# Narrower sums over the sequence in a fused attention and mixer kernel: 33 columns a head instead of 66, with a new hand-written order

## The chip, the core and the metric

The kernel runs on one core of one Trainium2 chip. The metric is the device time of one execution in microseconds (us); the kernel before has a median of 216.34 us over three runs (215.99 to 217.02). All arithmetic that matters here is in fp32 or in the faster fp32r form, and each engine (TensorE = PE, VectorE = DVE, ScalarE = ACT, GpSimd = POOL, SyncE = SP for the transfers) works through its own queue in order.

## What is computed

Linear attention with a second-order feature map over 4 batches of 4 heads, 1088 positions and 32 values a head, followed by a token mixer and a channel mixer:

```python
def phi(x):
    a = np.einsum('rd,bhsd->bhsr', S1, x)
    b = np.einsum('rd,bhsd->bhsr', S2, x)
    return np.einsum('bhsi,bhsj->bhsij', a, b).reshape(*x.shape[:-1], r * r)
q_p, k_p = (phi(q), phi(k))
kv = np.einsum('bhsf,bhsd->bhfd', k_p, v)
z = np.sum(k_p, axis=2)
num = np.einsum('bhsf,bhfd->bhsd', q_p, kv)
den = np.einsum('bhsf,bhf->bhs', q_p, z)[..., None] + 1e-06
x = num / den                       # then laid out as (batch, position, 128)
h = np.maximum(xt @ w_tok1, 0.0) @ w_tok2
u = x + h.transpose(0, 2, 1)
out = u + np.maximum(u @ w_ch1, 0.0) @ w_ch2
```

The change concerns `kv` and `z`: the sums over the sequence of 64 features times 32 values and a one.

## The kernel before

Every batch b goes through the same steps, and their names appear in the table ORDER, which is the program: `Plan.run` (L177) walks through it word by word and emits each step, so the order of words sets the order in every engine's queue. A word such as `~7` calls `fill` (L261), which puts that many matmuls of a zero tile into the PE queue where the order expects PE to wait.

- `K0` to `K3`, function `keys` (L425): projections of the keys (`.p`, L436, 64 columns moved), copies (`.c`, ACT), products on the DVE (`.v`, L466, in pieces of 4, 4 and 1 tiles of 128 positions), the sums (`.s`, L483), and the copy into `kvz` (`.kvz`, ACT L493). Batch 0 has the sums in six pieces, `K0.s00` to `K0.s18`; the others have one step.
- In the sums, each head h = 2p + j has nine matmuls, one for each tile of positions: 64 feature columns of `k_p` are the stationary side, and the result goes to partitions 0 to 63 (j = 0) or 64 to 127 (j = 1). The moving side is `v`, which holds 33 columns a head, 32 values and ones. Before, both heads of a pair move all 66 columns of the pair, so half of each result is never read: `blocks` (L491) copies only the head's own 33.
- `Q0` to `Q3`: query features; batch 0 on PE, ACT, DVE and POOL (L574 to L602), later ones through DRAM.
- `A0` to `A3`: `.x` (L692, attention), `.n`, `.r`, `.d` (division on ACT and DVE), `.t` (L752 or L758), `.relu`, `.hT`, `.w` (L874 or L878), `.u` (L783), and `.uh`, `.ul` (L849, L852), the two halves of u.
- `U0` to `U11`, spans of the channel mixer: `.f` (L928), `.h` (L932), `.l` (L935), `.s` (L941), three matmuls each for `.f` and `.s`.
- `w00` to `w32`: weights arrive as doubles and are rebuilt as fp32 by ACT (`.abs`, `.low`), DVE (`.clamp` L293, `.shift` L297, `.merge` L300) and POOL (`.add` L307, L309), then split in halves (`.hi`, `.lo`).
- LOADS is the order in which SP issues the first 25 transfers: `v0` is the values of batch 0, `03` the fourth piece of `w_tok1`, `15` the last of `w_tok2`.

Of the kernel before, what the change touches and what calls it, by code (L numbers as in the profile page):

```python
# [35 lines left out]
LOADS = "00 q0a 02 k0 q0b 01 v0 04 03 13 10 12 11 20 q1 k1 30 31 v1 21 15 14 32 22".split()  # L36
# [36 lines left out]
d12 K0.s10 K0.s14 K0.s18 w01.add d11 d20 K0.kvz ~2 A0.x0 w03.low q1 A0.n0 w10.abs A0.x1 A0.n1 k1 w04.merge A0.r0
A0.d0 d30 w04.low w04.add A0.r1 d31 w10.clamp@dve A0.d1 A0.x2 A0.t0 A0.n2 A0.t1 A0.r2 w03.add w10.shift A0.d2 Q1.p
w12.abs w11.abs w12.low v1 w20.abs w10.merge w12.clamp@dve w11.clamp@dve d21 d15 w10.low Q1.c0 w10.add Q1.c1 w11.low
w12.shift w13.abs d14 w20.clamp@dve d32 Q1.w0 Q1.w1 Q1.w2 w12.merge A0.t2 A0.relu ~2 A0.hT w12.add w30.abs d22
w11.shift w20.shift A0.hTh w11.merge w11.add w13.clamp@dve w20.merge w13.shift w20.low w20.add K1.p K1.c0
w30.clamp@dve K1.c4 w13.low w13.merge w13.add K1.v0 w30.low w20.hi w20.lo@pool w30.shift w30.merge w30.add A0.u0
A0.w0 A0.uh00 A0.u1 K1.c8 A0.ul00 A0.w1 U0.f w21.abs w31.low K1.v4 K1.v8 w21.clamp@dve U0.f U0.f K1.s w21.low
A0.uh11 A0.ul11 U0.h w30.hi w30.lo@pool U0.h U0.l U0.l w21.shift U0.h w31.abs w31.clamp@dve w15.abs U1.f U1.h A0.u2  # L80
w21.merge U0.l U0.s U1.f w21.add w31.shift w31.merge w31.add U0.s U0.s U1.l w22.low w22.abs U1.h U1.l U1.f U0.f
w21.hi w22.clamp@dve w21.lo@pool U1.h U1.l w31.hi w31.lo@pool U0.h w22.shift U0.l U1.s U1.s U1.s w22.merge w22.add
w32.abs U0.f U0.f U1.f w32.clamp@dve w04.hi U0.h U0.l U0.h U1.h w32.low w14.abs U0.s w15.clamp@pool U0.s U0.l
w32.shift w22.hi U0.s U1.f U1.l w32.merge w32.add U1.f U0.f w22.lo@dve U1.h U1.l U1.h U1.l U1.s w14.low w15.shift
U1.s U0.f U0.h w03.hi U0.h w14.clamp@pool U0.l w15.merge U0.l U1.s w14.shift U0.s w32.hi w32.lo@pool Q1.w3 U0.f U0.f
w14.merge w15.low U0.h U0.s w15.add U0.h U0.l w01.hi U0.l U0.f w00.hi U0.h U0.l w02.hi U0.f U1.f w14.add w00.lo@dve
U0.h w10.hi U0.s A0.w2 U1.h U1.l U0.s K1.kvz A0.uh22 U0.l U1.f w15.hi U0.oh@pool U1.h U0.s Q1.r0None Q1.r00 Q1.r01
# [965 lines left out]
```

## Time and profile before

| | value |
|---|---|
| median of the runs | 216.34 us |
| time of the profiled execution | 216.37 us |
| its span, first to last instruction | 213.9 us |
| instructions | 4865 |
| DMA traffic | 28.35 MB, mean 133 GB/s |

The profile divides the span in 40 slices of 5.3 us and lists groups of instructions by source line, the waits between engines and the chain of work that ended last. An fp32 matmul shows as two records on PE, so the 144 matmuls of the sums are 288 records. The stretch up to about 30 us, in which weights are loaded and rebuilt and the first batch goes through attention, is called the head below. Times inside the execution count from the span's start.

### The profile page before, as it was taken

To read this page: it belongs to the slowest core of one execution; us is meant where nothing else is said; L and a number is where in the kernel's file an instruction comes from. 1 tells how busy PE (TensorE), PEld (TensorE's weight loads), DVE (VectorE), ACT (ScalarE), POOL (GpSimd) and SP (SyncE) were. 2 spreads that over 40 slices of the span, in tenths; PEclk is the share of its full clock that TensorE was granted. 3 is DMA by queue.
4 is the path that set the end of the run, shared out by engine and by line. 5 is a ranking of instruction groups with operands and counts; after the bars stand their busy time and mean duration, and the time that the engine had idled before them with its cause. 6 is when DMAs were issued, how large, how long until landed. Compare 5 with 4: busy or idle time off the path is not lost.

```text
span 213.9 us, 4865 instructions
## 1 busy us (share of the span) xinstructions
PE 209.5 (98%) x1876; PEld 199.1 (93%) x1876; DVE 147.1 (69%) x299; ACT 116.2 (54%) x282; POOL 60.9 (28%) x66
## 2 busy tenths in 40 slices
PE   8999999999999999999999999999999999999993
PEld 7779779999998999999999999999999999999993
DVE  2899999998789765777434666585547656556562
ACT  4788997988456245444344544443336453544541
POOL 3177686989971001301000660010000010000000
PEclk9999999999999999999999999999999999999999
DMA  6999985750778598300697400014400200100000
GB/s 223 402 405 409 399 328 129 138 146 10 241 304 242 148 193 171 135 3 3 203 221 184 123 29 0 3 37 142 120 0 0 78 0 0 37 3 37 0 31 25
DMA packets 11398, 28.35 MB, mean 133 GB/s; under 512 B 1520, under 2 KB 5616, under 8 KB 11376
## 3 DMA queue, kind: packets, MB, share of 16 engines
q1 hardware_dynamic: 11232, 27.79, 41.7%
q8 instruction: 14, 0.23, 0.5%
q10 hardware_dynamic: 144, 0.26, 0.5%
q14 instruction: 8, 0.07, 0.1%
HBM read 23.21 MB, written 4.83 MB: 131 GB/s over the span
## 4 chain that ended last, share of the span: by engine, by line
PE 97%; ACT 1%; DVE 0%; issue 0%
PE ps_o L941 34%; PE ps_h L928 33%; PE ps_a L758 5%; PE ps_a L692 4%; PE ps_a L878 4%; PE ps_o L264 3%; PE ps_a L483 3%; PE ps_a L436 2%; PE ps_a L874 2%; PE ps_a L752 1%; PE ps_a L574 1%; PE ps_o L483 1%; PE ps_a L629 1%; PE ps_h L574 1%; PE ps_a L783 1%; PE ps_a L792 1%
## 5 line engine op out<-in xcount | busy, mean ns | idle before, releaser
L935 DVE SCALAR_TENSOR_TENSOR hl<-ps_h,hh 128x384 fp32r<-128x384 f32 (+2 forms) x144 | 74.5, 531 | 46.0 <-ACT hh L932 45.3
L932 ACT ACTIVATE hh<-ps_h 128x384 fp32r<-128x384 f32 (+2 forms) x144 | 67.4, 474 | 63.1 <-PE ps_h L928 54.0
L928 PE MATMUL ps_h<-uh,halves 128*128 128x384 f32 (+2 forms) x288 | 85.4, 330 | 0.0
L941 PE MATMUL ps_o<-hh,halves 128*128 128x384 f32 (+2 forms) x288 | 71.2, 330 | 0.0
L928 PEld LDWEIGHTS ps_h<-uh,halves 128*128 128x128 f32 x288 | 53.1, 188 | 0.6
L941 PEld LDWEIGHTS ps_o<-hh,halves 128*128 128x128 f32 x288 | 50.2, 188 | 0.8 <-issue 0.4
L928 PE MATMUL ps_h<-ul,halves 128*128 128x384 f32 (+2 forms) x144 | 47.1, 327 | 0.0
L941 PE MATMUL ps_o<-hl,halves 128*128 128x384 f32 (+2 forms) x144 | 47.1, 327 | 0.0
L852 POOL TENSOR_TENSOR ul<-us,uh 128x320 fp32r<-128x320 f32 (+4 forms) x10 | 7.2, 727 | 71.1 <-ACT uh L849 71.1
L928 PEld LDWEIGHTS ps_h<-ul,halves 128*128 128x128 f32 x144 | 27.1, 188 | 0.2 <-DVE ul L852 0.2
L941 PEld LDWEIGHTS ps_o<-hl,halves 128*128 128x128 f32 x144 | 27.1, 188 | 0.0
L307 POOL TENSOR_TENSOR whole<-c,tail 128x512 int32<-128x512 int32 (+3 forms) x11 | 11.7, 1072 | 2.7 <-ACT tail L290 1.3
L286 ACT ACTIVATE c<-doubles 128x512 f32<-128x512 f32 (+3 forms) x17 | 10.5, 625 | 3.1 <-DMA doubles<-wt 2.5
L466 DVE TENSOR_TENSOR k_p<-ps_a,a_sb 128x1024 f32<-128x1024 f32 (+1 forms) x12 | 11.0, 947 | 0.0
L722 POOL TENSOR_TENSOR xl<-x,xh 128x384 fp32r<-128x384 f32 x3 | 3.0, 1014 | 26.0 <-ACT xh L718 26.0
L290 ACT ACTIVATE tail<-doubles 128x512 int32<-128x512 uint32 (+3 forms) x17 | 10.4, 625 | 0.0
L300 DVE SCALAR_TENSOR_TENSOR c<-doubles,ps_h 128x512 int32<-128x512 int32 (+3 forms) x17 | 10.3, 609 | 0.2
L297 DVE TENSOR_SCALAR ps_h<-c 128x512 int32<-128x512 int32 (+3 forms) x17 | 10.2, 613 | 0.1
L758 PE MATMUL ps_a<-halves,xh 128*128 128x256 f32 x54 | 9.8, 283 | 0.0
L692 PEld LDWEIGHTS ps_a<-kvz,qp 128*64 128x64 f32 x288 | 8.7, 138 | 0.9 <-issue 0.7
L692 PE MATMUL ps_a<-kvz,qp 128*64 128x66 f32 x288 | 9.3, 223 | 0.0
L264 PE MATMUL ps_o<-still 128*128 128x128 f32 x38 | 8.0, 364 | 1.1 <-DVE still L242 1.1
(85 smaller groups left out, 238.7 us busy)
## 6 DMA issues: line engine op xcount, KB each, us to landing
qp<-rows SPq DMA_DIRECT2D x6, 544.0 KB, 5.0
br<-rows SPq DMA_DIRECT2D x12, 272.0 KB
doubles<-wc SPq DMA_DIRECT2D x6, 512.0 KB, 5.9
v_sb<-v SPq DMA_DIRECT2D x4, 594.0 KB, 10.6
doubles<-wt SPq DMA_DIRECT2D x4, 512.0 KB, 5.4
k_sb<-kT SPq DMA_DIRECT2D x3, 576.0 KB
xm<-xb SPq DMA_DIRECT2D x3, 576.0 KB
xT<-xm SPq DMA_DIRECT2D x12, 144.0 KB, 3.2
```

What stands on the lines that cost most here:

```text
L264: nc.tensor.matmul(spare_ps[:, :P], lhsT=still, rhs=still, start=True, stop=True)
L286: nc.scalar.activation(f32(t["c"]), f32(high), AF.Abs)
L290: nc.scalar.activation(t["tail"], low.bitcast(U32), AF.Copy, scale=2.0 ** -29)
L300: nc.vector.scalar_tensor_tensor(t["c"], high, -(1 << 30), t["ps"], op0=ALU.bitwise_and, op1=ALU.bitwise_or)
L307: engines[e].tensor_tensor(dst(), t["c"], t["tail"], op=ALU.add)
L466: engines["pool" if on_pool else "dve"].tensor_tensor(t["k_p"][:pn, t0 * H:t1 * H], a.unsqueeze(3).broadcast_to([pn, n, R, R]), t["sb", t0 ...
L692: nc.tensor.matmul(x_ps[c:c + 64, o:o + 2 * (D + 1)], lhsT=qp[:, p, s0 + c:s0 + c + 64], rhs=kvz_all[b % 2][:, p, :2 * (D + 1)], start=Tru ...
L758: nc.tensor.matmul(t["h_ps"][:, :DTOK], lhsT=t[l][:m, i, :], rhs=part(0, piece, r, j * DTOK, DTOK)[:m], start=(i == 0 and k == 0), stop=(i ...
L928: nc.tensor.matmul(h_ps[:, :cn], lhsT=part(2, at[2][e][0], l, at[2][e][1] * P, P), rhs=r[:, :cn], start=(m == 0), stop=(m == 2))
L932: nc.scalar.activation(t["hh"][:, :cn], t["h"][:, :cn], AF.Relu)
L935: nc.vector.scalar_tensor_tensor(t["hl"][:, :cn], t["h"][:, :cn], 0.0, f32(t["hh"][:, :cn]), op0=ALU.max, op1=ALU.subtract)
L941: nc.tensor.matmul(outs[i][:, :cn], lhsT=part(3, at[3][e][0], l, at[3][e][1] * P, P), rhs=r[:, :cn], start=(e == 0 and m == 0), stop=(e == ...
```

## The change

The sums move the head's own 33 columns and write them to the head's own 33 columns of the bank. The copy into `kvz` reads the same places as before. The planner's cost for one tile of a pair of heads is changed with it; these costs have no effect where ORDER is given. The table ORDER and the list LOADS are new from the first line to the last:

```diff
-LOADS = "00 q0a 02 k0 q0b 01 v0 04 03 13 10 12 11 20 q1 k1 30 31 v1 21 15 14 32 22".split()
+LOADS = "00 q0a 02 k0 q0b 01 03 04 v0 10 30 11 12 q1 13 20 k1 31 32 21 22 v1 14 15".split()
...
-v0 ~2 K0.s00 K0.s04 Q0.a10 K0.v8 K0.s08 Q0.m10 w01.shift w01.merge d04 d03 Q0.a11 Q0.b11 Q0.m11 w04.abs
...
+w03.clamp@dve v0 Q0.a21 K0.s00 K0.s04 w04.shift Q0.b21 Q0.m21 d10 Q0.a20 Q0.m20 w04.merge w01.add w03.shift
...
                         nc.tensor.matmul(
-                            t["kv"][j * F:(j + 1) * F, p * 2 * (D + 1):(p + 1) * 2 * (D + 1)],
+                            t["kv"][j * F:(j + 1) * F, h * (D + 1):(h + 1) * (D + 1)],
                             lhsT=t["k_p"][:n, i * H + h].rearrange("p i j -> p (i j)"),
-                            rhs=t["v"][:n, i, 2 * p:2 * p + 2, :].rearrange("p h d -> p (h d)"),
+                            rhs=t["v"][:n, i, h, :],
                             start=(i == 0), stop=(i == NT - 1),
                         )
...
-            last = plan.add(f"{n}.s", {"pe": 2 * NT * 117.0}, all_sums, ...
+            last = plan.add(f"{n}.s", {"pe": 2 * NT * 85.0}, all_sums, ...
...
-                    f"{n}.s{p}{t0}", {"pe": (t1 - t0) * 117.0}, sums(p, t0, t1), ...
+                    f"{n}.s{p}{t0}", {"pe": (t1 - t0) * 85.0}, sums(p, t0, t1), ...
```

What the new order does to the queues is shown at three places. The first is PE between the second query projection and the first attention of batch 0. L574 are the query projections, L264 the fills, L483 the sums of batch 0, L692 the attention. Before:

```order
L264 MATMUL ps_o<-still 128x128 x3
L574 MATMUL ps_a<-q_sb,s_spread 128x384 x2
L574 MATMUL ps_h<-q_sb,s_spread 128x384 x2
L264 MATMUL ps_o<-still 128x128 x2
L483 MATMUL ps_o<-v_sb,k_p 64x66 x18
L574 MATMUL ps_a<-q_sb,s_spread 128x320 x2
L574 MATMUL ps_h<-q_sb,s_spread 128x320 x2
L483 MATMUL ps_o<-v_sb,k_p 64x66 x18
L264 MATMUL ps_o<-still 128x128 x2
L692 MATMUL ps_a<-kvz_84,qp 64x66 x36
```

The same place on PE after the change:

```order
L264 MATMUL ps_o<-still 128x128 x2
L574 MATMUL ps_a<-q_sb,s_spread 128x384 x2
L574 MATMUL ps_h<-q_sb,s_spread 128x384 x2
L264 MATMUL ps_o<-still 128x128 x7
L574 MATMUL ps_a<-q_sb,s_spread 128x320 x2
L574 MATMUL ps_h<-q_sb,s_spread 128x320 x2
L483 MATMUL ps_o<-v_sb,k_p 64x33 x36
L264 MATMUL ps_o<-still 128x128 x2
L692 MATMUL ps_a<-kvz_84,qp 64x66 x36
```

The half of the sums that stood ahead of the third query projection now follows it, and seven fills stand where two fills and that half stood.

The second place is the DVE around the first reciprocal (L704) of batch 0; L293, L297 and L300 are conversions of weights, L712 a division. Before:

```order
L300 SCALAR_TENSOR_TENSOR c<-doubles_94,ps_h 128x512
L300 SCALAR_TENSOR_TENSOR c<-doubles_93,ps_h 128x256
L704 RECIPROCAL rec<-den 128x12
L712 TENSOR_TENSOR x<-ps_a,rec 128x384
L704 RECIPROCAL rec<-den 128x12
```

And after:

```order
L300 SCALAR_TENSOR_TENSOR c<-doubles_93,ps_h 128x512
L293 TENSOR_SCALAR c<-c 128x384
L704 RECIPROCAL rec<-den 128x12
L712 TENSOR_TENSOR x<-ps_a,rec 128x384
L704 RECIPROCAL rec<-den 128x12
```

One clamp of 384 columns has come ahead of the reciprocal; before, it follows it.

The third place is the DVE ahead of the first `ul` (L852), with which the channel mixer can begin; L466 are products of the keys of batch 1. Before:

```order
L300 SCALAR_TENSOR_TENSOR c<-doubles_95,ps_h 128x384
L466 TENSOR_TENSOR k_p<-ps_a,a_sb 128x1024
L297 TENSOR_SCALAR ps_h<-c 128x512
L300 SCALAR_TENSOR_TENSOR c<-doubles_100,ps_h 128x512
L852 TENSOR_TENSOR ul<-ps_a,uh 128x384
```

And after:

```order
L466 TENSOR_TENSOR k_p<-ps_a,a_sb 128x1024
L293 TENSOR_SCALAR c<-c 128x512
L297 TENSOR_SCALAR ps_h<-c 128x512
L466 TENSOR_TENSOR k_p<-ps_a,a_sb 128x256
L300 SCALAR_TENSOR_TENSOR c<-doubles_96,ps_h 128x512
L852 TENSOR_TENSOR ul<-ps_a,uh 128x384
```

The small product of 256 columns now stands ahead of `ul`; before, it follows. The clamp of 512 columns stands ahead of `ul` in both, before the change a few rows earlier. On PE, two fills more stand ahead of the second pair of L874 matmuls (`A0.w1`), and the sums of batch 1 stand right behind the third group of L783 instead of apart from it. After the head PE keeps the same work in another interleaving.

More of the change, by code (lines that the diff above doesn't have):

```diff
@@ L73 @@
[L73 to L87, printed above, removed]
@@ L123 @@
-U10.l U10.f U10.s U10.h U10.l U10.f U10.h U10.l U10.l U10.f U10.s U10.l U11.f U10.s U10.s U10.h U10.l U11.f U10.s
-U11.f U11.h U11.h U11.h U11.l U11.l U10.s U11.s U11.f U11.f U11.s U10.ol U10.out U11.l U11.h U11.h U11.f U11.h U11.s
-U11.l U11.f U11.l U11.f U11.s U11.s U11.l U11.s U11.f U11.h U11.h U11.l U11.f U11.s U11.l U11.f U11.s U11.h U11.h
-U11.l U11.l U11.f U11.s U11.h U11.h U11.s U11.l U11.l U11.s U11.s U11.ol U11.out
+s k0a s.abs s.clamp s.shift s.low s.merge s.add s.rows ~4 K0.p0 d00 w00.abs q0a w00.clamp@dve Q0.s0@pool Q0.s1@pool
@@ new lines @@
+~1 Q0.p0 d02 K0.c0 K0.v0 w00.low w02.abs k0 ~1 K0.p4 w00.shift w02.low Q0.a00 w02.clamp@dve w00.merge w00.add Q0.a01
+Q0.b01 q0b K0.c4 K0.c8 d01 w01.abs w01.low Q0.m00 ~2 Q0.p1 Q0.m01 Q0.a10 w02.shift K0.v4 w02.merge w02.add Q0.a11
+Q0.b11 Q0.m11 w01.clamp@dve K0.v8 d03 d04 w04.abs w03.abs Q0.m10 w03.low w01.shift w01.merge ~7 Q0.p2 w04.clamp@dve
+w03.clamp@dve v0 Q0.a21 K0.s00 K0.s04 w04.shift Q0.b21 Q0.m21 d10 Q0.a20 Q0.m20 w04.merge w01.add w03.shift
+w03.merge d30 d11 w03.add d12 q1 d13 K0.s08 K0.s10 w10.abs w10.clamp@dve K0.s14 K0.s18 K0.kvz ~2 A0.x0 w04.low A0.x1
@@ new lines @@
+w22.hi w22.lo@pool U1.f U1.h U1.h U0.f U0.h w14.clamp@dve U1.l U1.l w15.shift U0.l w15.merge w15.add U1.s U1.s U0.f
+U0.h w14.shift w12.hi U0.l w14.merge w14.add U1.s U0.s U0.f U0.f w32.hi U0.f U0.h w32.lo@dve K1.kvz U0.h w10.hi U0.h
+U0.l U0.s U0.s U0.f U0.h U0.l U1.f U0.l U0.oh@dve A0.w2 Q1.w0 Q1.w1 Q1.w2 Q1.w3 w03.hi Q1.r0None Q1.r00 Q1.r01
+Q1.r1None Q1.m10@pool Q1.r10 Q1.r11 w11.hi U0.l q2 U1.f k2 Q1.m11@pool v2 q3 U0.s U1.f U1.h A0.uh22 U1.h U0.s U0.s
+U1.l A0.ul22 U1.f U1.h w04.hi Q1.m01@dve w01.hi U1.h Q1.m00@pool w02.hi A1.x U1.l U1.f U1.l U1.l w02.lo@pool A1.n1
@@ L522, in all_sums @@
                     sums(p, 0, NT)(_)
-            last = plan.add(f"{n}.s", {"pe": 2 * NT * 117.0}, all_sums, products + [v_loaded[b]], [kv_hold], [kp_hold, v_hold[b]], boost, 1)
+            last = plan.add(f"{n}.s", {"pe": 2 * NT * 85.0}, all_sums, products + [v_loaded[b]], [kv_hold], [kp_hold, v_hold[b]], boost, 1)
         for p in () if b else range(2):
```

89 lines of the change are left out of this document (49 added, 40 removed).

## The prediction

> **What bounds the kernel now.** I read the page first, then the chain of work that ended last, then the timeline of the head. The page's busy shares, and PE and DVE in 40 slices of 5.3 us:
>
> ```profile
> PE 209.5 (98%) x1876; PEld 199.1 (93%) x1876; DVE 147.1 (69%) x299; ACT 116.2 (54%) x282; POOL 60.9 (28%) x66
> PE   8999999999999999999999999999999999999993
> DVE  2899999998789765777434666585547656556562
> GB/s 223 402 405 409 399 328 129 138 146 10 241 304 242 148 193 171 135 3 3 203 221 184 123 29 0 3 37 142 120 0 0 78 0 0 37 3 37 0 31 25
> ```
>
> PE is busy all along, but in the head that share deceives, since fills count as busy there. DVE is at 9 tenths or near it over the first eight slices, and the transfers run at some 400 GB/s until 27 us. So the head is set by several engines together, and the rest by PE alone. Whatever PE saves behind the head is time saved; what it saves inside the head counts only where DVE waits for it.
>
> The chain, in order of time (start, length, line, records), where the sums (L483) and their neighbours stand:
>
> ```profile
> 9.41 0.86 PE ps_o L264 x6
> 10.28 0.84 PE ps_a L574 x4
> 11.12 0.65 PE ps_h L574 x4
> 11.77 0.64 PE ps_o L264 x4
> 12.41 1.20 PE ps_o L483 x36
> 13.61 0.74 PE ps_a L574 x4
> 14.35 0.54 PE ps_h L574 x4
> 14.89 1.20 PE ps_o L483 x36
> 16.09 0.64 PE ps_o L264 x4
> 16.73 2.25 PE ps_a L692 x72
> ...
> 31.12 2.25 PE ps_a L483 x72
> 33.37 0.72 PE ps_h L928 x3
> ...
> 34.94 0.52 PE ps_h L928 x3
> ...
> 55.85 2.25 PE ps_a L692 x72
> ...
> 62.21 1.20 PE ps_a L436 x36
> ...
> 66.86 2.25 PE ps_a L483 x72
> 69.12 1.05 PE ps_a L436 x36
> ...
> 99.43 2.25 PE ps_a L483 x72
> ```
>
> **What a sum costs, and what sets its pace.** 36 records cost 1.20 us and 72 cost 2.25, so 36 more cost 1.05: 29.2 ns a record, or 58.3 for a pair, one record on each half of the partitions, side by side. Four batches take 2.40 + 3 x 2.25 = 9.15 us. Would half the columns be half of that? L436, the projections of the keys, tells:
>
> ```profile
> L436 PE MATMUL ps_a<-s_blocks,k_sb 128*64 128x64 f32 x144 | 5.7, 235 | 0.0
> L483 PE MATMUL ps_a<-v_sb,k_p 128*64 128x66 f32 x216 | 7.0, 223 | 0.0
> ```
>
> The form 128*64 is the weights' rows and columns, 128x64 or 128x66 what is moved. L436 has the same 64 columns of weights and moves 64 columns, not 66. Its 36 records cost 1.20 with the entry, like those of the sums, and 1.05 right behind the sums. If the moved columns set the pace, 36 records would take 1.05 x 64/66 = 1.02, a difference of 0.03 that rows of two decimals would show. It isn't there, so something common to both sets the pace: 64 columns of weights. The sums in the third batch, and L629 ahead of them, give the size of that (min, median, max in ns):
>
> ```profile
> L483 PE MATMUL ps_a<-v_sb,k_p x72: 220/222/273, 66.8 to 68.9; 128*64 128x66 f32 x72
> ...
> L629 PE MATMUL ps_a<-q_sb,s_rows x16: 387/403/418, 66.2 to 66.5; 64*32 64x272 f32 x16
> ```
>
> The record that begins a block waits for its own weights with nothing to cover them: 273 - 222 = 51 ns for 64 columns, and about 418 - 387 = 31 for 32. In the middle of a block one load must end before the next can start, so 51 ns a pair is a floor whatever is moved, and 58.3 is what a pair takes. I bound the new pair from both sides: 58.3 (weights set the pace throughout) and 58.3 x 33/66 = 29.2 (moved columns do after all). Between them stands 51. I take 58.3, because the equality of 64 and 66 columns speaks for it and the floor of 51 lies near it. Each block may end one narrower record earlier, at most 0.03 us.
>
> TensorE: Matmul & The Clock Gate of the Trainium skill, Part 3, on what overlaps, says that a weight load overlaps a matmul in flight only where the two use different groups of rows; all pairs here use all 128 rows. By that rule load and moved columns would add up, and 33 columns fewer would save the full 29.2 ns a pair, the extreme of the first rival below; the trace speaks against it, since a load of 51 plus 66 columns would need over 58.3.
>
> **The head.** First the PE queue, which now has one fill less, the second query projection, seven fills, the third projection, all sums, two fills, attention. The rows that the start of each piece depends on, from the timeline:
>
> ```profile
> 12.78 0.54 DVE L602 TENSOR_TENSOR qp<-xT,ps_h 128x384 f32<-128x384 f32 x1
> 16.14 0.43 ACT L493 COPY kvz<-ps_o 64x66 f32<-64x66 f32 x2 [0.44 <-PE ps_o L483]
> 17.84 0.23 DVE L704 RECIPROCAL rec<-den 128x12 f32<-128x12 f32 x1 [0.39 <-ACT den L700]
> 18.78 0.30 DVE L293 TENSOR_SCALAR c<-c 128x384 f32<-128x384 f32 x1
> 12.45 0.41 DVE L466 TENSOR_TENSOR k_p<-ps_a,a_sb 128x256 f32<-128x256 f32 x1
> 27.67 0.31 PEld L783 LDWEIGHTS ps_a<-ident,x 128*128 128x128 f32 x3 [0.49 <-DVE k_p L466]
> 28.85 0.55 DVE L852 TENSOR_TENSOR ul<-ps_a,uh 128x384 fp32r<-128x384 f32 x1
> ```
>
> And the stretch up to `ul` in the view by windows (busy us and instructions of PE, PEld, DVE, ACT and POOL, then clock, DMA share and GB/s):
>
> ```profile
> 5.80:28.85 23.05, 23.00 (x297) 17.16 (x296) 22.33 (x46) 19.15 (x48) 14.55 (x14) 1.00 1.03 403
> ```
>
> Two records of fill are 0.86 - 0.64 = 0.22. The second projection ends at 11.77 or 0.22 earlier. Fourteen fill records are 0.64 + 5 x 0.22 = 1.74, which ends at 13.29 to 13.51. The third projection needs the bank that L602 frees at 12.78 + 0.54 = 13.32, so the fills cover that wait. It runs 0.74 + 0.54 = 1.28, to about 14.7. All sums in one block are 2.25, to 16.95 (two blocks were 2.40). The two fills that cover the copy into `kvz` are 0.64, as before. Attention starts at about 17.6, where it started at 16.73: **+0.85**. Values `v0` now land behind `03` and `04`, 768 KB at 405 GB/s or 1.9 us later; before, they were there at 12.41 at the latest, so now by 14.3, ahead of 14.7. That hides the later load; if the cover goes, the excess goes on top.
>
> Then DVE. It had waited 0.39 for the first `den`; with attention 0.85 later, the reciprocal comes at 18.7. Behind it stand in order the divisions and all conversions up to `ul`, so they all shift. One clamp of 384 (0.30, or 0.22 net, since neighbours overlap by 0.08) is now done inside that wait, and one product of 256 (0.41, 0.33 net) has come ahead of `ul`. The window up to `ul` has DVE busy for 22.33 of 23.05 us, so there is no slack to absorb it. `ul` starts at 28.85 + 0.85 - 0.22 + 0.33 = 29.8: +0.95. PE gives the same: its wait of 0.49 at L783 goes, as PE arrives later than that product, and two new fills (0.43 to 0.64) stand where it was. I take **+0.95** for the start of the channel mixer; from below 0, if the loads that arrive otherwise let DVE and PE catch up, from above 1.6, by the third rival.
>
> **Behind the head.** The shares of the chain by engine:
>
> ```profile
> PE 97%; ACT 1%; DVE 0%; issue 0%
> ```
>
> So a delay at 30 us is carried to the end.
> - Sums of batches 1 to 3: 3 x 36 pairs x (58.3 - 58.3) = 0, and at the ends 4 x 0.03 = 0.1 saved.
> - The block of batch 1 no longer stands alone among L928. A return to L928 cost 0.72 instead of 0.52, so one return fewer saves 0.2.
> - `v1` is issued behind three more loads of 512 KB (`21`, `32`, `22`), 3.9 us at 405 GB/s. It was issued at 16.13 and took 10.6 to land, 26.7, so it lands at 30.6. Its sums start at 31.12 + 0.95 plus some 0.4 for L783 ahead of them: hidden, by 1.8 us.
>
> ```profile
> 16.13 0.33 SPq L268 DMA_DIRECT2D v_sb<-v  x1
> v_sb<-v SPq DMA_DIRECT2D x4, 594.0 KB, 10.6
> ```
>
> - The rows of queries 1, written by SP, now queue behind all loads, up to 32 us. Attention of batch 1 reads them at 55.85 in the chain; hidden.
> - The end keeps its form, a last `.s`, one addition and one transfer: 0.
>
> **The sum**, against the profiled execution's own 216.37 us (a span of 213.9 and 2.47 around it, and 0.03 from the median): 216.37 + 0.95 - 0.1 - 0.2 = **217.0**, a change of +0.3%. A measurement of this kernel tells about 0.5%, or 1.08 us, from no change, so the edges are 215.3 and 217.4.
>
> **Rivals.**
> 1. *The moved columns count after all.* At 29.2 a pair, 36 pairs save 1.05 us a batch: three batches behind the head 3.15, and batch 0 takes the same off the delay of 0.95: 217.0 - 4.2 = 212.8. The planner's cost fell from 117 to 85 for two pairs; 117 is 2 x 58.3, so 85 may have been seen as well. 42.5 a pair would save 36 x 15.8 ns = 0.57 a batch, four times: 217.0 - 2.3 = 214.7, the price I give this rival. For it: that number, and that PE is never idle behind the head. Against it: L436 at the same pace with 64 columns, and 42.5 is less than the 51 of a lone load. Chance 0.28, of which 0.05 for the extreme.
> 2. *A floor of its own.* With 51 a pair, 7.3 ns x 36 x 4 = 1.05: 216.0. TensorEngine Tiling of the Trainium skill, Instruction Overhead, has a matmul of one column as long as one of 60; by it 33 columns would save what 66 to 60 does, 58.3 x 6/66 = 5.3 ns a pair or 0.8 in four batches, and the time would be 216.2. No run here shows so few columns. Chance 0.12, together with a head that catches up (216.1).
> 3. *Slower: the late sums hold up the head further.* The place is the start of attention. If the fills run at the 0.16 a record of the group of four, fourteen take 2.24, not 1.74, and attention starts at 18.1; the two fills ahead of L874 then add their 0.15 to 0.2 in full. The delay is 1.6 instead of 0.95: 217.7. It decides when attention starts after 18.0. For it: the rate of the group of four; against it: the group of six. Chance 0.15.
>
> **How the numbers follow.** The forecast, 216.5 to 217.5, has 0.45. The range goes from 214.4, which takes in most of the first rival, to 217.9, past the third. It leaves out the extreme of the first, 212.8, and a head that loses over 1.7. Faster by over 0.5%: most of the first rival, 0.23. Slower by over 0.5%: the third rival and the upper edge of the forecast, 0.22. The rest, 0.55, is within 0.5%.
>
> **What would show it.** In the changed profile, the 288 records of L483 should stand 29 ns apart, with blocks of 2.2 to 2.3 us; blocks of 1.6 would mean the first rival, 1.9 the second. Attention of batch 0 should start at 17.4 to 17.8, the first reciprocal wait a microsecond, and `ul` start at 29.6 to 30.0. What would make it wrong: a pair faster than 51 ns, attention that starts by 17.0, or a new wait of PE behind 35 us, which I have at none.

## The result, and the profile after

| | before | after |
|---|---|---|
| median of the runs compared | 216.17 us (4 runs) | 218.63 us (4 runs) |
| time of the profiled execution | 216.37 us | 218.56 us |
| its span | 213.9 us | 216.6 us |

The change makes the kernel slower: the ratio is 1.0112, with a 95% interval of 1.007 to 1.0153. The measured time lies 1.6 us above the forecast of 217.0 and 0.7 above its range.

The page after, busy shares and the two rows in slices, and the shares of its chain by engine:

```profile
PE 210.5 (97%) x1888; PEld 199.7 (92%) x1888; DVE 144.4 (67%) x294; ACT 116.6 (54%) x282; POOL 65.9 (30%) x71
PE   8899999999999999999999999999999999999993
DVE  2898999897787554877533866755736755555563
...
PE 90%; DMA 5%; DVE 2%; ACT 1%; issue 0%; SPq 0%
```

PE looks as busy as before. The chain tells more: DMA and DVE now hold 7% of it, where DVE had 0%. Somewhat under half of that stands in the first 9 us, in the loading and rebuilding of the first weights; the rest comes later. The chain of the kernel after, in order of time (start, length, line, records):

```profile
11.79 1.76 PE ps_o L264 x14
...
14.82 2.22 PE ps_o L483 x72
...
17.69 2.25 PE ps_a L692 x72
...
29.62 1.29 PE ps_a L874 x4
30.92 1.82 PE ps_h L928 x9
33.06 2.22 PE ps_a L483 x72
35.28 0.73 PE ps_o L941 x3
...
64.97 6.17 DMA k_sb<-kT
...
71.27 1.27 PE ps_a L436 x36
...
131.37 1.21 DVE qp L672
```

The sums of a batch take 2.22 us, where they took 2.25: half the moved columns, the same block. Attention starts 0.96 later than before, the channel mixer (L928) 1.41 later (30.92 against 29.51). Its piece in the chain before:

```profile
29.51 1.61 PE ps_h L928 x9
```

Then a load of keys and a product on DVE stand in the chain, far behind the head. The chain counts the whole length of such a piece, the 6.17 of the load for example; how long PE waited for it stands in another view. The view of PE's waits from 35 us to the end (engine, line, what it waited for: us in total, times, longest) lists three, and none of them is in the kernel before:

```profile
PE ps_a L436 <- DMA k_sb<-kT: 0.3, 1, 0.3
PE ps_a L483 <- PE ps_a L629: 0.3, 1, 0.3
PE ps_h L928 <- DVE hl L935: 0.2, 1, 0.2
```

To see where time is lost, PE's own work without the fills was added up record by record, each at the usual pace of its kind, and each kernel's time at the same amount of work was set against that of the kernel before. This loss is a number worked out from the traces, for one profiled execution of each kernel. The table gives it at 40 us and at 210 us of the kernel before; "behind" is what was added between. "Time" is the median of all runs of a kernel, "spans" that of the runs less than 1.5% above its fastest. "Old" and "new" are the orders; the head ends where the first channel mixer step begins.

| kernel | time | spans | attention | `ul` | loss at 40 | at 210 | behind |
|---|---|---|---|---|---|---|---|
| before | 216.05 to 216.81 | 214.0 to 214.2 | 16.66 | 28.85 | 0 | 0 | 0 |
| after | 218.63 | 216.7 | 17.62 | 30.47 | 1.58 | 2.76 | 1.18 |
| e1: old order, 33 columns | 216.32 | 213.9 | 16.89 | 29.12 | 0.66 | 0.68 | 0.02 |
| e2: new order, 66 columns | 218.81 | 216.8 | 17.85 | 30.70 | 1.83 | 2.85 | 1.02 |
| h1: old head, new rest | 219.13 | 217.0 | 16.54 | 28.97 | 0.54 | 2.02 | 1.48 |
| h2: new head, old rest | 217.03 | 215.15 | 17.46 | 30.31 | 1.41 | 1.23 | -0.18 |
| g1: k3 later | 218.62 | 216.7 | 17.72 | 30.56 | 1.67 | 2.75 | 1.08 |
| g2: product later | 218.50 | 216.6 | 17.57 | 30.41 | 1.53 | 2.20 | 0.67 |
| g12: both | 218.83 | 216.6 | 17.87 | 30.73 | 1.82 | 2.48 | 0.66 |
| i1: loads behind the store | 218.19 | 216.25 | 16.91 | 29.75 | 0.87 | 1.94 | 1.07 |
| i2: old head, g1, g2, i1 | 217.39 | 215.25 | 17.71 | 29.94 | 1.53 | 2.01 | 0.48 |
| j1: new head, four undone | 218.15 | 216.2 | 17.52 | 30.36 | 1.47 | 2.28 | 0.81 |
| j2: old head, four undone | 217.16 | 215.0 | 16.35 | 28.59 | 0.15 | 0.81 | 0.66 |
| k1: new head, three undone | 217.30 | 215.3 | 17.55 | 30.40 | 1.51 | 1.54 | 0.03 |
| k2: old head, three undone | 216.96 | 214.8 | 16.44 | 30.87 | 3.12 | 3.04 | -0.08 |
| j3: product behind `ul` | 216.87 | 215.1 | 17.57 | 30.21 | 1.34 | 1.18 | -0.16 |
| f1: two fills | 218.97 | 217.05 | 17.14 | 30.55 | 1.66 | 3.43 | 1.77 |
| f2: values earlier | 220.64 | 218.7 | 17.77 | 31.78 | 3.68 | 5.10 | 1.42 |

### The profile page after: what moved, and what is told of

Its sections match the earlier page's. It is cut to its first block, busy times and chain, and to the rows that moved or that the text cites. A ratio compares the mean times of both kernels' runs of the same rounds, so it can differ in the third digit from the quotient of the medians.

```text
span 216.6 us, 4887 instructions
## 1 busy us (share of the span) xinstructions
PE 210.5 (97%) x1888; PEld 199.7 (92%) x1888; DVE 144.4 (67%) x294; ACT 116.6 (54%) x282; POOL 65.9 (30%) x71
## 4 chain that ended last, share of the span: by engine, by line
PE 90%; DMA 5%; DVE 2%; ACT 1%; issue 0%; SPq 0%
PE ps_o L941 32%; PE ps_h L928 32%; PE ps_a L758 4%; PE ps_a L692 4%; PE ps_a L878 4%; DMA k_sb<-kT 3%; PE ps_a L436 2%; PE ps_a L483 2%; DMA doubles<-wt 2%; PE ps_a L752 2%; PE ps_o L264 2%; PE ps_a L874 2%; PE ps_o L483 1%; PE ps_a L574 1%; PE ps_a L783 1%; PE ps_a L629 1%
## 5 line engine op out<-in xcount | busy, mean ns | idle before, releaser
L935 DVE SCALAR_TENSOR_TENSOR hl<-ps_h,hh 128x384 fp32r<-128x384 f32 (+2 forms) x144 | 74.3, 532 | 46.9 <-ACT hh L932 46.3
L928 PE MATMUL ps_h<-uh,halves 128*128 128x384 f32 (+2 forms) x288 | 86.0, 331 | 0.2 <-DVE hl L935 0.2
L941 PE MATMUL ps_o<-hh,halves 128*128 128x384 f32 (+2 forms) x288 | 71.0, 329 | 0.0
L928 PEld LDWEIGHTS ps_h<-uh,halves 128*128 128x128 f32 x288 | 53.0, 188 | 1.3 <-DVE hl L935 0.7
L941 PEld LDWEIGHTS ps_o<-hh,halves 128*128 128x128 f32 x288 | 50.1, 188 | 0.6 <-issue 0.4
L928 PE MATMUL ps_h<-ul,halves 128*128 128x384 f32 (+2 forms) x144 | 47.1, 327 | 0.0
L941 PE MATMUL ps_o<-hl,halves 128*128 128x384 f32 (+2 forms) x144 | 47.0, 327 | 0.0
L928 PEld LDWEIGHTS ps_h<-ul,halves 128*128 128x128 f32 x144 | 27.1, 188 | 0.5 <-DVE ul L852 0.5
L852 POOL TENSOR_TENSOR ul<-us,uh 128x256 fp32r<-128x256 f32 (+4 forms) x11 | 7.9, 720 | 63.6 <-ACT uh L849 63.3
L941 PEld LDWEIGHTS ps_o<-hl,halves 128*128 128x128 f32 x144 | 27.1, 188 | 0.0
L307 POOL TENSOR_TENSOR whole<-c,tail 128x512 int32<-128x512 int32 (+3 forms) x11 | 12.5, 1141 | 9.6 <-DVE c L300 7.8
L466 DVE TENSOR_TENSOR k_p<-ps_a,a_sb 128x1024 f32<-128x1024 f32 (+1 forms) x12 | 11.2, 951 | 0.7 <-ACT a_sb L446 0.7
L409 POOL TENSOR_TENSOR halves<-whole,halves 128x512 fp32r<-128x512 f32 (+3 forms) x9 | 10.0, 1125 | 5.2 <-ACT halves L406 5.2
L297 DVE TENSOR_SCALAR ps_h<-c 128x512 int32<-128x512 int32 (+3 forms) x17 | 10.4, 616 | 0.1
L300 DVE SCALAR_TENSOR_TENSOR c<-doubles,ps_h 128x512 int32<-128x512 int32 (+3 forms) x17 | 10.3, 611 | 0.1
L264 PE MATMUL ps_o<-still 128*128 128x128 f32 x50 | 9.2, 335 | 1.1 <-DVE still L242 1.1
L264 PEld LDWEIGHTS ps_o<-still 128*128 128x128 f32 x50 | 7.9, 235 | 2.4 <-issue 1.1
L722 POOL TENSOR_TENSOR xl<-x,xh 128x384 fp32r<-128x384 f32 x5 | 5.1, 1016 | 15.1 <-ACT xh L718 15.1
```

Of the source, the lines that this page charges most:

```text
L264: nc.tensor.matmul(spare_ps[:, :P], lhsT=still, rhs=still, start=True, stop=True)
L297: nc.vector.tensor_scalar(t["ps"], t["c"], 3, 0x3FFFFFFF, op0=ALU.logical_shift_left, op1=ALU.bitwise_and)
L300: nc.vector.scalar_tensor_tensor(t["c"], high, -(1 << 30), t["ps"], op0=ALU.bitwise_and, op1=ALU.bitwise_or)
L307: engines[e].tensor_tensor(dst(), t["c"], t["tail"], op=ALU.add)
L466: engines["pool" if on_pool else "dve"].tensor_tensor(t["k_p"][:pn, t0 * H:t1 * H], a.unsqueeze(3).broadcast_to([pn, n, R, R]), t["sb", t0 ...
L928: nc.tensor.matmul(h_ps[:, :cn], lhsT=part(2, at[2][e][0], l, at[2][e][1] * P, P), rhs=r[:, :cn], start=(m == 0), stop=(m == 2))
```

## Experiments: sums or order

The change has two parts that do not need each other. Each alone:

```diff
 e1: ORDER and LOADS of before
-rhs=t["v"][:n, i, 2 * p:2 * p + 2, :].rearrange("p h d -> p (h d)"),
+rhs=t["v"][:n, i, h, :],
 e2: ORDER and LOADS of after
-rhs=t["v"][:n, i, h, :],
+rhs=t["v"][:n, i, 2 * p:2 * p + 2, :].rearrange("p h d -> p (h d)"),
```

> The kernel before with its own order and loads; only the sums move 33 columns instead of 66. Theory (64 columns of weights set the pace, so the narrower side is hidden): pairs of records in L483 stay 58.3 ns apart, the time is that of before within 0.3 us, at most 0.1 us less. Rival (the moved columns count somewhere that the changed profile does not show, such as at the ends of the blocks): 215 us or less with before at 216.2.

> The changed kernel with its new order and loads, but 66 columns moved. Theory: the order alone makes the loss, so the time is that of the changed kernel, 218.6 us, within 0.3 us, and pairs stay at 58.3 ns. Rival (the narrower sums save something and the order loses more than the whole): 219.5 us or more.

e1 measured 216.32 us, ratio 0.9978 (0.9943 to 1.0012); e2 218.81, ratio 1.0088 (1.0055 to 1.012). Narrow sums alone gain nothing that shows, and the new order alone makes the loss. In e1 the 36 records of a half batch and the 72 of a batch stand in the timeline (start, length, then the form) as

```profile
15.07 1.24 PE L483 MATMUL ps_o<-v_sb,k_p 128*64 128x33 f32 x36
31.33 2.29 PE L483 MATMUL ps_a<-v_sb,k_p 128*64 128x33 f32 x72
```

so 18 pairs more take 1.05 us: 58.3 ns a pair, as with 66 columns. In the records themselves 33, 64 (L436) and 66 columns all come to 58.33.

## Experiments: what sets the pace of a pair

Two runs change one size of the pair each, in the order of before. e3 is e1, with its 33 moved columns, and takes 32 of the 64 feature columns as weights, so half of the features are left out of the sums. e4 is the kernel before, with all 64, and moves the columns of all four heads.

```diff
 e3
-lhsT=t["k_p"][:n, i * H + h].rearrange("p i j -> p (i j)"),
+lhsT=t["k_p"][:n, i * H + h, :R // 2].rearrange("p i j -> p (i j)"),
 e4
-rhs=t["v"][:n, i, 2 * p:2 * p + 2, :].rearrange("p h d -> p (h d)"),
+rhs=t["v"][:n, i].rearrange("p h d -> p (h d)"),
```

> Only as a measurement of the pace: the order of before, 33 columns moved, and 32 of the 64 feature columns as weights, so that half of the features are left out of the sums. Theory (the load of the weights' columns sets the pace of a pair): the pair falls from 58.3 ns to 29 to 35, and the 72 records of a batch from 2.2 to about 1.2 us. Rival (a fixed pace of some 58 ns for a pair whatever its sizes): 58.3 as before. Second rival (the rows of the weights or the moved columns set the pace, not the weights' columns): 58.3 too, or anything above 45.

> The other side of the same measurement: the order of before, 64 feature columns as weights, and the 132 columns of all four heads moved, of which three heads' are not read. Theory (the slower of weight load and moved columns sets the pace, and 66 columns lie just under the load): the pair rises to 110 to 117 ns, 132 columns at 58.3/66 = 0.88 ns each or somewhat less, and the time by 36 x 4 pairs x 55 ns = 8 us less what the head hides: 222 to 225. Rival (load and moved columns add up, and the equality of 33, 64 and 66 is a floor): above 125. Second rival (a fixed pace whatever is moved): 58.3 and 216.3.

The timeline of e3, a half batch and a batch:

```profile
14.68 0.76 PE L483 MATMUL ps_o<-v_sb,k_p 128*32 128x33 f32 x36
31.17 1.33 PE L483 MATMUL ps_a<-v_sb,k_p 128*32 128x33 f32 x72
```

and of e4:

```profile
16.10 2.25 PE L483 MATMUL ps_o<-v_sb,k_p 128*64 128x132 f32 x36
70.99 4.27 PE L483 MATMUL ps_a<-v_sb,k_p 128*64 128x132 f32 x72
```

With half the weights 18 pairs take 0.57 us, 31.7 ns a pair; with 132 moved columns 2.02 us, 112.2 (112.5 in the records themselves). One run each: 214.31 us for e3 and 224.35 for e4, 8 us above before as expected. So a pair takes the longer of two things: the load of its weights, 31.7 ns for 32 columns and 58.3 for 64, or its moved columns, 112.5 / 132 = 0.85 ns each. By that 66 columns are 56 ns, just under the 58.3 of their weights, which is why the halving found nothing to save. All rivals with a fixed pace, and the one in which load and columns add up, fall.

The rule that the prediction took from TensorE: Matmul & The Clock Gate of the Trainium skill, Part 3, its list of what overlaps (a load overlaps a matmul in flight only where the groups of rows differ), falls with them for this case: all rows are in use in every pair, and 33 columns or 66 make the same 58.3 ns. The floor of some 60 columns in TensorEngine Tiling of the Trainium skill, Instruction Overhead, does not show here either: 33 columns pass in 31.7 ns once the weights let them.

## Experiments: which part of the order

The order was cut at the first step of the channel mixer, and the head of one joined to the rest of the other.

```diff
 h1
 ORDER up to the first U0.f, LOADS: before
+ORDER from the first U0.f: after
 h2
 ORDER up to the first U0.f, LOADS: after
+ORDER from the first U0.f: before
```

Steps that only the other order has ahead of the cut stand right ahead of it: six in h1, three in h2.

> 33 columns. All steps up to the first step of the channel mixer stand in the order of before, with its loads; what is left follows in the new order. Theory (the loss has two parts, 1.6 us in the head and 1.2 us behind it, at the sums of batch 2, the keys of batch 3 and a wait for hl at 133 us): 217.2 to 217.5 us. Rival (the waits behind the head only follow from a head that ends late): 216.2 us, like before.

> 33 columns. The new order and loads up to the first step of the channel mixer, and what is left in the order of before. Theory (two parts): 1.6 us over before, 217.6 to 217.9 us. Rival (all comes from the head): 218.6 us.

h1: 219.13 us, ratio 1.0099 (1.0061 to 1.0137). h2: 217.03, ratio 1.0012 (0.9983 to 1.004), and no wait of PE behind the head. By the spans the new head alone costs about 1.0 (215.15 against 214.2), and the new rest behind it another 1.55 (216.7 against 215.15). The loss is not all in the head. Nor do the two parts simply add: behind the old head the new rest loses 2.8 (217.0 against 214.2), more than behind the new one, with runs from 215.5 to 218.2.

## Experiments: the places behind the head

Three waits are in the profile after, a fourth in that of h1. Moved one by one:

```diff
 g1
-K3.p A1.l1@pool ... K3.c8 A1.t0
+A1.l1@pool ... A1.t0 K3.p K3.c8
 g2
-U5.l Q3.m10@dve U5.l U5.s U5.f U5.l Q3.m01@pool
+U5.l U5.l U5.s U5.f U5.l Q3.m10@dve Q3.m01@pool
 g12: both
 i1
-U0.l q2 U1.f k2 Q1.m11@pool v2 q3 U0.s ... A1.x ... U0.ol ... U0.out
+U0.l U1.f Q1.m11@pool U0.s ... U0.ol U0.out q2 k2 v2 q3 A1.x
 i2: the old head of h1, with g1, g2 and i1
```

> The changed kernel with the first keys step of batch 3 (its projections and its first copy) moved behind the token mixer's first matmul step of batch 1 (.t0), so that PE has its other work to do while the load of k3 is under way. Theory (the wait for k3 near 71 us is a cost of the new order, and nothing behind it is hidden): the 0.3 of wait that L436 has there goes, and with the return to L928 that it forces the time falls by 0.3 to 0.5 us: 218.1 to 218.3 where the changed kernel has 218.6. Rival (the wait only takes the place of the wait for DVE right ahead of it, sums of batch 2 for K2.v8, so PE waits there all the same): within 0.2 of the changed kernel, with a wait of 0.3 or more on DVE or on ps_a in its place between 68 and 75 us.

> The changed kernel with one query product of batch 3 (Q3.m10 on DVE, 1.21 us) moved behind the next two low halves of the channel mixer's hidden values (L935) that it now stands ahead of. Theory (PE's wait at 133 us for hl is due to that product on the DVE queue): the waits of 0.16 on PE and 0.48 on PEld at 133 us go, and the time falls by 0.3 to 0.5: 218.1 to 218.3. Rival (those hl wait for ACT or for PE's own spans, not for the product): the same wait stands, time within 0.2 of 218.6. A second rival: the product in its new place holds up the two hl behind it, and the wait appears some 1.5 us later at the same size.

> Both moves together. Theory (two separate waits of PE, one behind the other on the path): the gains add up to 0.7 to 1.0 us: 217.6 to 217.9. Rival (PE's lost time is made up later whatever the wait, since some later event has a time of its own): the gain of both together is no more than that of the better one alone.

> The changed kernel with the loads of batch 2 and 3 (q2, k2, v2, q3) moved back behind the store of the first span of the channel mixer (U0.out, with its addition U0.ol), both ahead of the attention of batch 1, which is where the kernel before has them in SP's queue. In the changed kernel these loads are issued from 37.4 to 40.6 us, while the rows of the queries of batch 1 are being read, and in the kernel before from 54.3 on. Theory (the loads share the transfers with those reads, and in part of the executions the reads end too late for the attention of batch 1, as in the profiled run with k3 later, which lost 0.38 there): the reads end by 51 us as before, the waits at 53 to 56 us are gone in every run, the time falls by 0.3 to 0.6 to 218.0 to 218.3, and the runs lie within some 1 us of each other, where those of the new order spread over 1.6 to 2.9. Rival (the reads take their 15 us by themselves, being small pieces): they end at 52 as before the move, and the time stays within 0.2 of 218.6. Slower is possible too, if k2 then lands after 64 us, where its projections start.

> Narrow sums, the old head, and the new order behind the head with all three repairs: loads of batch 2 and 3 behind the first store, k3's projections later, the query product of batch 3 later. The old head with the new rest alone has 219.1. Theory (the three places behind the head, queries of batch 1, k3 and the product at 133 us, are the whole loss of the new order's rest): within 0.5 of the kernel before run beside it, 216.0 to 217.0. Rival (the new rest is tight throughout, and each wait taken away lets another appear): 217.5 to 219.0, with waits of PE of 0.2 or more at places that the changed kernel's profile does not show.

**The product (g2).** The time is 218.50, 0.1 below the kernel after, less than hoped and within what the runs can tell. The profile does show the mechanism. The timeline after, DVE, POOL and PE around 133 us:

```profile
129.32 2.68 POOL L672 TENSOR_TENSOR qp<-qp,br 128x544 f32<-128x544 f32 x2 [0.98 <-DMA br<-rows]
131.37 1.21 DVE L672 TENSOR_TENSOR qp<-qp,br 128x544 f32<-128x544 f32 x1
132.50 1.56 DVE L935 SCALAR_TENSOR_TENSOR hl<-ps_h,hh 128x384 fp32r<-128x384 f32 x3
133.10 0.45 PE L928 MATMUL ps_h<-uh,halves 128*128 128x384 f32 x1 [0.16 <-DVE hl L935]
```

and in g2, where the product has moved behind POOL's:

```profile
129.28 2.69 POOL L672 TENSOR_TENSOR qp<-qp,br 128x544 f32<-128x544 f32 x2 [1.05 <-DMA br<-rows]
...
132.82 0.72 DVE L672 TENSOR_TENSOR qp<-qp,br 128x544 f32<-128x544 f32 x1
```

The same product of 544 columns takes 1.21 us beside POOL's and 0.72 behind it. In the first case it ends at 132.58, 0.58 after POOL's pair ends at 132.00; in i1, where it starts earlier, it takes 1.51 and ends 0.57 after. In g1 it starts only 0.25 before POOL's pair ends, takes 0.83, and ends 0.58 after. So it waits for POOL to finish, whenever it starts, and three low halves (L935) queue behind it in the kernel after. SBUF — State Buffer of the Trainium skill, Who interferes with whom, has a DVE instruction with two inputs in SBUF contend with a GpSimd instruction that reads SBUF, and calls the ports that they share an exclusive lock. The trace agrees: 0.72 alone, 0.83, 1.21 and 1.51 together. In the profiles the loss at this place is 0.44 after and 0 in g2; without the move it is 0.05 in g1 and 0.75 in i1, by how early the product starts.

**k3 (g1).** 218.62, nothing gained. g12: 218.83, nothing gained by both. The k3 wait goes, but j1 and k1 below, which differ in this move alone, show that the move itself costs 0.9 of span (216.2 against 215.3).

**The loads (i1).** 218.19, ratio 1.0092 (1.0055 to 1.0129); the spans fall by 0.45, within what was expected. The queue of SP tells why. Before, q2, k2, v2 and q3 stand behind the store of the first span, which waits for the channel mixer:

```profile
53.93 0.36 SPq L977 DMA_DIRECT2D outT<-o_sb  x1
54.34 0.43 SPq L268 DMA_DIRECT2D q_sb<-qT  x1
```

After, they are issued while the rows of the queries of batch 1 are still being read:

```profile
36.15 1.20 SPq L662 DMA_DIRECT2D br<-rows  x2
37.39 0.44 SPq L268 DMA_DIRECT2D q_sb<-qT  x1
```

The profiled execution after does not lose by it. That of g1, with the same four loads in the same place, does; its timeline has POOL waiting for the reads, and PE's weights for POOL:

```profile
52.99 3.17 POOL L672 TENSOR_TENSOR qp<-qp,br 128x544 f32<-128x544 f32 x2 [1.73 <-DMA br<-rows]
...
56.22 2.18 PEld L692 LDWEIGHTS ps_a<-kvz,qp 128*64 128x64 f32 x72 [0.63 <-POOL qp L672]
```

In i1 POOL has its reads at 49.10 and there is no such wait. The expected narrow spread did not come: eight of the twelve runs lie between 215.7 and 216.4 of span, the others reach 217.3 and more. The store and its addition (U0.ol, L960) move too, so the gain of i1 is not of the loads alone: in its profile k3 is there in time without any move of K3.p, and the store no longer goes out just ahead of that load.

**All three (i2).** 217.39, ratio 1.0048 (1.0017 to 1.0079): better than the 219.13 of h1, but not the 216.0 to 217.0 of the theory. Its profile has one place left, which the profile after has as well (timeline after, keys of batch 2):

```profile
64.28 0.55 DVE L960 TENSOR_TENSOR o_sb<-o_sb,ps_o 128x384 f32<-128x384 f32 x1 [0.28 <-POOL o_sb L957]
...
68.14 0.42 DVE L466 TENSOR_TENSOR k_p<-ps_a,a_sb 128x256 f32<-128x256 f32 x1 [0.25 <-ACT a_sb L446]
...
68.67 2.29 PE L483 MATMUL ps_a<-v_sb,k_p 128*64 128x33 f32 x72 [0.28 <-PE ps_a L629]
```

The wait is put down to PE's own L629; what came last was the small product, at 68.14 + 0.42 = 68.56. An addition for a store (L960), with a wait of its own for POOL, stands ahead of the products of this batch on DVE and holds them all up. So the addition of the second store was moved behind the products as well, and, when that still left a loss, k3 was put back:

```diff
 j1, j2: new head, old head; g1, g2, i1, and
-U1.ol ... K2.c0 K2.v0 ... K2.c4 K2.v4
+K2.c0 K2.v0 ... K2.c4 K2.v4 U1.ol
 k1, k2: the same without g1
-A1.t0 K3.p K3.c8
+K3.p A1.l1@pool ... K3.c8 A1.t0
```

> The changed kernel (new head) with four places behind the head undone: loads of batches 2 and 3 behind the first store, k3's projections behind .t0 of batch 1, the query product of batch 3 later, and the addition of the second span's store (U1.ol) behind the products of the keys of batch 2 instead of ahead. Theory (these four places are the whole loss behind the head): the span falls from 216.7 to that of the new head with the old rest, 215.15, within 0.4, the time to 217.0 to 217.5. Rival (some of the loss is spread over gaps that no one place explains): the span stays at 215.7 or more, the time at 217.7 or more, and in its profile the loss against the kernel before still grows by 0.3 or more between 36 and 210 us.

> The same with the old head: the kernel with three places undone (span 215.25 in the middle of its runs) and the fourth, the store's addition, moved behind the products. Theory (four places): the span falls by 0.3 at 68 us alone and to within 0.5 of the kernel before, 214.1 to 214.7, the time 216.3 to 216.9. Rival (spread): 215.0 or more, time 217.1 or more.

> The changed kernel with the loads of batches 2 and 3 behind the first store, the query product of batch 3 later, and the second store's addition behind the products of the keys of batch 2; k3's projections stay where the change puts them. Theory (these three places make the loss behind the head; k3 is in time once its load is issued earlier): span 215.0 to 215.5, at the new head with the old rest (215.15), time 216.9 to 217.4; the loss against the kernel before grows by no more than 0.2 between 36 and 210 us. Rival (spread): span 215.8 or more.

> The same with the old head. Theory: span 213.8 to 214.4, as the kernel before, time 215.9 to 216.5, where the old head with the untouched new rest has 217.0 and 219.1. Rival (spread): span 214.8 or more, time 216.9 or more.

j1: 218.15 us; j2: 217.16. Both miss: the wait for the small product is gone, but PE has a new one right behind the sums, which the kernel after has not. The timeline of j1:

```profile
69.21 1.01 POOL L409 TENSOR_TENSOR halves<-whole,halves 128x384 fp32r<-128x384 f32 x1
69.44 1.13 DVE L409 TENSOR_TENSOR halves<-whole,halves 128x320 fp32r<-128x320 f32 x1 [1.59 <-ACT halves L406]
70.49 0.48 DVE L935 SCALAR_TENSOR_TENSOR hl<-ps_h,hh 128x320 fp32r<-128x320 f32 x1
71.02 0.42 PE L928 MATMUL ps_h<-uh,halves 128*128 128x320 f32 x1 [0.51 <-DVE hl L935]
```

Two splits of weights (L409) meet on DVE and POOL; POOL was first, and DVE's takes 1.13. In the kernel after DVE's is first, at 69.81, and takes 0.49, while POOL's takes 1.28 instead of 1.01. The low half behind it comes late, and with k3's projections moved away (g1) PE has nothing else to do ahead of it. The loss at this place grows by 0.9 in both. k1, without that move: 217.30, ratio 1.0028 (0.9999 to 1.0057), span 215.3, near the 215.15 of h2, with no wait in the view of PE's waits behind 35 us and a loss that grows by 0.03. **Three moves together take the loss behind the head away**: the loads (with the first store and its addition) back in their places, the second store's addition behind the keys' products, the product on DVE behind POOL's. What each is worth alone is not shown: i1 gained 0.45 of span, g2 0.1, and the second store's addition was never moved alone. k2 has the same rest, and its profile agrees (-0.08 behind the head), but its time, 216.96 with a ratio of 1.0047 (1.0015 to 1.0079), is above the 216.5 expected. Its spans go from 213.8 to 216.9, and the profiled one lost 3.1 before 40 us; in it PE waits 0.57 for a load of queries at 22 us and 1.37 for the keys' product ahead of L783 at 29.7. By the count of the table all four old heads with the new rest also lose 0.4 or more between 34 and 38 us, just behind the cut (0.12 to 0.55 in h1). What the other runs of k2 lost was not seen, and stays open.

## Experiments: the head

```diff
 f2
-LOADS = "00 q0a 02 k0 q0b 01 03 04 v0 10 30 ..."
+LOADS = "00 q0a 02 k0 q0b 01 v0 03 04 10 30 ..."
-~7 Q0.p2 ... K0.s00 K0.s04 ... K0.s08
+~2 K0.s00 K0.s04 K0.s08 Q0.p2
 f1
-~7 Q0.p2
+~2 Q0.p2
 j3: h2, and
-K1.v8 w30.merge w30.add A0.u0 A0.w0 A0.uh00 A0.ul00 A0.u1 ~2 A0.w1
+w30.merge w30.add A0.u0 A0.w0 A0.uh00 A0.ul00 K1.v8 A0.u1 A0.w1
```

> The changed kernel with the head's sums put back: v0 is loaded ahead of 03 and 04, the first half of the sums of batch 0 (K0.s00, .s04, .s08) stands ahead of the third query projection again, and two fills stand in the place of seven. Everything else of the new order stays. Theory (the fills and the late sums set the start of the first attention, and with it the channel mixer's): attention of batch 0 starts at 16.7 to 17.0 instead of 17.69, and the time falls by 0.6 (0.3 to 1.0): 217.6 to 218.3. Rival (the DVE's new row of conversions and the pieces of weights that arrive in another order set the start of ul, whatever PE does ahead of it): attention starts earlier, but ul starts within 0.3 of where it does now and the time stays within 0.3 of 218.6.

> The changed kernel with two fills instead of seven ahead of the third query projection. Theory (the fills only cover the wait for the bank that the product on DVE frees, and the sums wait for the values' load besides): PE waits in their place, the third projection starts within 0.1 us as long after the second as now (3.25 us from start to start), and the time stays within 0.3 of 218.6. Rival (the fills hold PE up): the projection comes 0.3 to 1.0 earlier, and the time falls by as much, to 217.6 to 218.3.

> The new head with the old rest, with the product of 256 columns of the keys of batch 1 (K1.v8) moved behind the first ul, where the kernel before has it, and without the two fills ahead of the second pair of L874. Theory (that product and those fills make the 0.62 that the new head loses between 25 and 30 us): the loss there falls to 0.3 or less, the first ul starts 0.3 to 0.4 earlier, and the time falls from 217.03 by 0.3 to 0.6 to 216.4 to 216.7. Rival (ul is late because the rebuilt weights are, or because attention is): the loss between 25 and 30 us stays at 0.5 or more and the time within 0.2 of 217.0.

f2 lost 2 us more: 220.64. Attention did not start earlier (17.77), and the waits from 9 to 36 us say why:

```profile
ACT c L286 <- DMA doubles<-wt: 2.4, 3, 1.1
...
PE ps_a L692 <- ACT kvz L493: 1.0, 1, 1.0
```

With the values ahead, the pieces of weights land later, ACT waits 2.4 us for them (0.9 after), and the copy into `kvz` stands behind them on ACT. So the late values are not a cost to take away by themselves: what comes ahead of them is waited for too. f2 tells nothing of the fills.

f1 does. With two fills, the first half of the third projection starts 2.32 us after the second instead of 3.25; its other half waits for L602, and the sums and attention follow 0.3 earlier, counted from the second projection. The fills do hold PE up, against the theory. But the time, 218.97, does not fall, against the rival; it is even just above the 218.9 that the theory allowed. `ul` starts at 30.55, no earlier than with seven. This profile does not show why: PE stands for 0.68 in the middle of the attention, for nothing that the profile shows, so the keys' projections of batch 1 come 0.5 later than after, and DVE's product waits 0.18 for their copy. What `ul` would do without that stop stays open.

The other profiles point to DVE for `ul`. From attention to `ul` every old head but that of k2 takes 12.2 to 12.4 us, and every new head but f1, f2 and j3 takes 12.84 to 12.86. The DVE row of the head of after, the first reciprocal and the last pieces ahead of `ul`:

```profile
18.80 0.23 DVE L704 RECIPROCAL rec<-den 128x12 f32<-128x12 f32 x1 [0.61 <-ACT den L700]
...
25.24 1.15 DVE L297 TENSOR_SCALAR ps_h<-c 128x512 int32<-128x512 int32 x2
26.30 1.14 DVE L300 SCALAR_TENSOR_TENSOR c<-doubles,ps_h 128x512 int32<-128x512 int32 x2
...
29.55 0.42 DVE L466 TENSOR_TENSOR k_p<-ps_a,a_sb 128x256 f32<-128x256 f32 x1
29.88 0.68 DVE L300 SCALAR_TENSOR_TENSOR c<-doubles,ps_h 128x512 int32<-128x512 int32 x1
30.47 0.55 DVE L852 TENSOR_TENSOR ul<-ps_a,uh 128x384 fp32r<-128x384 f32 x1
```

Before, the shifts and merges at this place are mostly of 384 columns:

```profile
22.75 1.14 DVE L297 TENSOR_SCALAR ps_h<-c 128x384 int32<-128x384 int32 x2
23.81 0.54 DVE L300 SCALAR_TENSOR_TENSOR c<-doubles,ps_h 128x384 int32<-128x384 int32 x1
```

Between the first reciprocal and `ul` DVE has 25 instructions in both kernels. But three of the L297 and L300 have 512 columns where they had 384, at 0.14 each (0.68 against 0.54), next to the one product more and the one clamp less. That is 0.42 + 0.33 - 0.27 = 0.48, of the 0.66 by which the stretch grew (11.01 to 11.67). No run put the three conversions back, so their share is read from the profile and not shown by an experiment. j3 takes the product and two fills away: `ul` is 0.21 closer to attention, but the time is 216.87 us, 0.16 below h2 and within the 0.2 of the rival, and the spans hardly differ (215.1 against 215.15). The loss between 25 and 30 us is still 0.49, of 0.68 in h2. The loads of L874's weights on PE tell why, first after, then in j3:

```profile
29.82 0.48 PEld L874 LDWEIGHTS ps_a<-whole,hTl 128*128 128x128 f32 x2 [0.17 <-POOL whole L307]
29.75 0.30 PEld L874 LDWEIGHTS ps_a<-whole,hTl 128*128 128x128 f32 x2 [0.61 <-POOL whole L307]
```

Without the fills they wait 0.61 for POOL's rebuilt weights (L307), with them 0.17 behind 0.45 of fills: the fills only cover a wait that is there anyway.

## Why the prediction failed, step by step

- **What a sum costs: right.** 58.3 ns a pair, blocks of 2.22, e1 without a measurable gain. The reason was right as well, and e3 and e4 show it on both sides. The first rival, at 0.28 the largest, fell, and so did the second. A lone load as a bound was not contradicted: 51 read and 58.3 measured for 64 columns, 31 read and 31.7 measured for 32.
- **The start of attention: right in size, not wholly in reason.** Forecast +0.85, measured +0.96, and 17.62 lies in the 17.4 to 17.8 that was to show it. That the fills only cover the wait for L602 was wrong by 0.3 (f1). The first reciprocal waits 0.61, not the microsecond that was to show it.
- **From attention to `ul`: wrong.** The term "28.85 + 0.85 - 0.22 + 0.33" has +0.1 for DVE between the reciprocal and `ul`; measured is 0.66. The step counted the two instructions whose place changed and took the rest as the same, while three conversions in between had become wider (0.42 of it, by the profile alone). The wait of 0.49 at L783, said to go, is still there (0.52), and what stands behind it is a wait for POOL's rebuilt weights, which the step did not have and which the two fills cover. `ul` came at +1.62, the third rival's delay of 1.6, but attention started at 17.6, not after 18.0: another mechanism than that rival's. In all runs together the new head costs less than in this one profile, about 1.0 of span (h2).
- **Behind the head: wrong, and the larger part.** The step has "hidden", "a new wait of PE behind 35 us, which I have at none", and a gain of 0.3. Measured are 1.18 in the profile, 1.55 by the spans. The 0.03 at the end of a block came; the return that was to be saved did not, for what follows the sums of batch 1 still takes 0.73 (L941 at 35.28). It looked at where the sums, v1 and the written rows had moved, but not at the four loads that now leave ahead of the first store, at the stores' additions on DVE, or at which products of DVE and POOL fall side by side. k1 takes three moves back and loses no more than 0.03 behind the head.
- **The sum.** The forecast kept 2.47 us around the span; after the change it is 1.9 to 2.0 in all four runs, which hid 0.5 of the loss. That 2.47 belonged to the one execution that was profiled: the middle of all runs of the kernel before is 2.06 to 2.08. In the profiled executions 0.65 was forecast and 2.19 measured, about 0.6 missed in the head (1.58 for 0.95), 1.5 behind it (1.18 for -0.3), less that 0.5.

No version beats both kernels beyond what the runs can tell. The old order with 33 columns (e1) is level with the kernel before.

## What to carry to other kernels

Fewer moved columns save nothing where the weights' load sets the pace; change the number of weight columns once, and the moved columns once, and the longer of the two is known. When a whole order is replaced, look at every queue behind the part that the change is about: which loads have come ahead of a store that used to hold them back, what stands on DVE ahead of the product that PE waits for, and which large instructions of DVE and POOL now meet. A delay that is taken away counts only if the next instruction that is waited for is early too: j1 and j3 moved one wait and met the next.

## What was not expected of the hardware

- One head order starts attention anywhere from 16.35 to 17.71 us in six profiled executions (the old head in before, e1, h1, i2, j2 and k2). Where it started last, in i2, the chain of the head begins with a transfer of the queries:

```profile
1.65 5.60 DMA q_sb<-qT
```

  The order of the loads is the same in all of them; what delays a transfer there was not studied. Differences of less than a microsecond in the head are therefore read from the medians, or from stretches inside one execution.
- An instruction of DVE with two inputs in SBUF that meets one of POOL waits for its end: 0.83, 1.21 and 1.51 us for a product that takes 0.72 alone, 1.13 for a split that takes 0.49. Which of the two engines comes first decides which one pays, so a move of half a microsecond elsewhere can put 0.6 on the engine that PE waits for.
